# Two pairs of tiles change places in on-chip memory: the key tiles ahead of the token tiles

## The chip, the cores and the metric

The kernel runs on one core of a Trainium2 chip. Its engines are TensorE (matrix products; in the profile PE for the products and PEld for loading their weights), VectorE (DVE), ScalarE (ACT) and GpSimd (POOL); SyncE (SP) issues the DMA transfers. On-chip memory has 128 partitions; a tile takes the same range of bytes in each of them, and "a byte offset" here is the place of that range inside a partition. The metric is the time of one execution on the device, in microseconds.

## The reference

Everything is float32. Two layers follow an attention stage:

```
# attention: batch 2, 8 heads, 768 tokens, 64 channels a head
k_sum = max of k over blocks of 32 tokens;  v_sum = mean of v over the same blocks
scores = q k^T / 8 where |i - j| < 16 (else -1e9), beside q k_sum^T / 8 + log 32
x = softmax(scores) [v; v_sum]                      -> 1536 tokens x 512
# layer 0 and layer 1: 512 -> 2048 -> 512
h = x @ w_in;   g = h * clip(h + 3, 0, 6) / 6;   x = g @ w_out
h = x @ w_in2;  g = h * sigmoid(h);              out = g @ w_out2
```

## The kernel before

**Precision.** Each float32 operand of the two layers is split into a high and a low part (fp32r), and each product is made of three matmuls: high by high, high by low, low by high.

**Tiling.** The 1536 tokens are three blocks `j` of 512. Each layer's 2048 inner channels are two halves of 8 groups `f` of 128. A step is one (layer, half, j, f): there are 2 x 2 x 3 x 8 = 96. `hidden` (line 682) makes the 128 x 512 inner activations of a step with 12 matmuls: 4 blocks `kk` of 128 input channels by the three pairs of parts. ScalarE and VectorE then apply the activation and split the result (`act`, `gate`, `gate_hi`, `gate_lo`, lines 693 to 711). `project` (lines 732 and 735) adds the step's product with `w_out` to accumulators in PSUM with 12 matmuls. `finish` empties them into `acc` tiles (lines 775 to 789), from which the next layer's tokens are split (lines 785 and 793) or the output is written.

**Order.** One list, `ORDER`, written out in the file, gives the order of all operations, and so each engine's own order. Attention for 24 windows of 64 queries is woven into the first steps of layer 0. The weights are converted to high and low parts by ScalarE, VectorE and GpSimd (lines 380 to 420) as they arrive.

**The tiles of the change.** The token tiles `x1_0` and `x1_1` hold the tokens of blocks j = 0 and 1 for layer 0; in layer 1 the same bytes are `x2_0` and `x2_1`. The third block lies elsewhere, in a tile called `late` (`x1_late` in layer 0, `x2_2` in layer 1). All have the shape

```
x_shape = [P, WIDE // SUB, 2, KD, SUB]      # 128, 2 token halves, high/low, 4 blocks kk, 256 tokens
```

so that a partition holds 16,384 bytes of one, and a matmul of line 682 reads, as its moving operand,

```
w[:, a, kk * P : (kk + 1) * P],             # stationary: 128 x 128 weights
x[:, :, b, kk, :],                          # moving: two runs of 256 floats
```

two runs of 1,024 bytes that begin 8,192 bytes apart, the first at the tile's start + 4,096 b + 1,024 kk. Lines 732 and 735 read their moving operand (`g` or `w`) as one run of 2,048 bytes. The key tiles `kT` (12,608 bytes) hold the transposed keys of the two batches; GpSimd and VectorE copy windows out of them (line 565). Their bytes become the `acc` tiles (12,288 bytes, same tags `ka0`, `ka1`) later. No matmul reads `kT` or `acc`.

The trace leaves buffer numbers out of names. Its `x` is `x1_0`, `x1_1`, `x2_0`, `x2_1` and also `x2_2`; its `x_late` is `x1_late`.

Of the kernel before, what the change touches and what calls it, by code (L numbers as in the profile page):

```python
# [11 lines left out]
F32R = mybir.dt.float32r  # L12
# [8 lines left out]
P = 128  # L21
# [9 lines left out]
KD = DM // P  # L31
NF = DFF // P
HALF = NF // 2
WIDE = 512
NWIDE = NT // WIDE
SUB = 256
# [285 lines left out]
def attention_moe_kernel(  # L322
# [13 lines left out]
    main = ctx.enter_context(tc.tile_pool(name="main", bufs=1))  # L336
    psum = ctx.enter_context(tc.tile_pool(name="psum", bufs=1, space=bass.MemoryType.PSUM))

    def ring(pool, name, n, shape, dtype=F32):
        return Ring([pool.tile(shape, dtype, tag=f"{name}{i}", name=f"{name}{i}") for i in range(n)])  # L340

    cst = main.tile([P, NCONST], F32, tag="cst", name="cst")
    ident = cst[:, :P]
    x_shape = [P, WIDE // SUB, 2, KD, SUB]
    x1 = [main.tile(x_shape, F32R, tag=f"x{j}", name=f"x1_{j}") for j in range(NWIDE - 1)]
    kT = [main.tile([P, NHP * KROW + PAD], F32, tag=f"ka{b}", name=f"kT{b}") for b in range(B)]

    def key_rows(b, o=0):
        return kT[b][:, o : o + NHP * KROW].rearrange("p (h t) -> p h t", h=NHP)

    mags = ring(main, "mag", 1, [P, DM])
    bitss = ring(main, "bits", 2, [P, DM], U32)
    words = ring(main, "words", 3, [P, 2 * DM], U32)
# [564 lines left out]
```

## Time and profile before

| | |
|---|---|
| median of 3 runs | 627.41 us (625.96 to 627.69) |
| profiled execution | 626.98 us, of which 625.2 us from the first to the last instruction (the span) |
| PE busy | 608.6 us, 97% of the span |
| DVE busy | 398.8 us, 64% |
| ACT busy | 243.4 us, 39% |
| POOL busy | 63.4 us, 10% |
| mean granted TensorE clock | 0.989 of full |

Matmuls are pipelined, so that the busy time of one (some 390 ns) is longer than the distance to the next. The rate is read from starts: the start of one row of the timeline minus the start of the row before it, divided by the matmuls of that row.

### The profile page before, as it was taken

Reading aid. Unit: us, or ns where it says so; the run is one execution under the profiler, and the core shown is the slowest. Engines: PE = TensorE matmul, PEld = TensorE weight load, DVE = VectorE, ACT = ScalarE, POOL = GpSimd, SP = SyncE. Lnnn points to the kernel's source line nnn. Section 1 sums busy time; section 2 is a strip of 40 time slices with the busy share of each in tenths; the row PEclk is TensorE's granted clock in tenths of the full one; section 3 lists DMA queues with packets and bytes.
Section 4 is the critical chain, followed back from the end, with each engine's and each line's share of the span. In section 5 each row is a group of like instructions: output and inputs, shape, how many; then the busy total and the mean of one; then the engine's idle time right before and its main releaser. Section 6 shows DMA issues by size and latency. Waiting matters only on the chain.

```text
span 625.2 us, 8645 instructions
## 1 busy us (share of the span) xinstructions
PE 608.6 (97%) x3208; PEld 500.3 (80%) x3208; DVE 398.8 (64%) x908; ACT 243.4 (39%) x568; POOL 63.4 (10%) x90
## 2 busy tenths in 40 slices
PE   6899999999999989999999999999999999999997
PEld 5788788888788868888888888888888888888886
DVE  5789999856569999862369999432159423332442
ACT  3789787454235454331143453211243221111100
POOL 3576443111010000000000000000000000000000
PEclk8799999999999998999999999999999999999999
DMA  9997854221324454400003434200003000100101
GB/s 240 208 225 179 226 158 141 80 60 26 92 67 135 143 161 136 150 17 1 1 0 102 139 107 128 66 0 1 0 1 101 1 1 1 68 0 1 68 1 67
DMA packets 69051, 51.56 MB, mean 82 GB/s; under 512 B 36369, under 2 KB 63505, under 8 KB 69009
## 3 DMA queue, kind: packets, MB, share of 16 engines
q1 hardware_dynamic: 69008, 51.01, 28.9%
q8 instruction: 25, 0.41, 0.3%
q14 instruction: 18, 0.14, 0.1%
HBM read 47.85 MB, written 3.15 MB: 82 GB/s over the span
## 4 chain that ended last, share of the span: by engine, by line
PE 82%; DVE 13%; ACT 3%; issue 1%; POOL 0%; ACTq 0%; DVEq 0%
PE bank L682 37%; PE bank L735 21%; PE bank L732 18%; DVE bits L398 2%; DVE bits L405 2%; PE bank L575 2%; PE bank L644 1%; DVE bits L385 1%; DVE mag L392 1%; PE bank L632 1%; PE bank L470 1%; ACT prob L604 1%; DVE rw L700 1%; DVE gw L711 1%; PE bank L851 1%
## 5 line engine op out<-in xcount | busy, mean ns | idle before, releaser
L682 PE MATMUL bank<-x,w 128*128 128x512 f32 x720 | 179.2, 396 | 0.7 <-DVE x L667 0.7
L682 PEld LDWEIGHTS bank<-x,w 128*128 128x128 f32 x720 | 133.7, 188 | 30.9 <-ACT early_units L604 0.9
L735 PE MATMUL bank<-w,gw 128*128 128x512 f32 (+1 forms) x456 | 103.8, 378 | 0.0
L735 PEld LDWEIGHTS bank<-w,gw 128*128 128x128 f32 x456 | 82.9, 188 | 16.8
L711 DVE TENSOR_TENSOR gw<-rw,gw 128x512 fp32r<-128x512 f32 x80 | 55.1, 689 | 49.2 <-ACT gw L707 47.5
L704 DVE TENSOR_TENSOR rw<-bank,rw 128x512 f32<-128x512 f32 x48 | 32.9, 686 | 69.3 <-ACT rw L695 69.3
L380 ACT ACTIVATE mag<-words 128x512 f32<-128x512 f32 x64 | 43.3, 676 | 65.4 <-DVE bits L398 65.2
L695 ACT ACTIVATE rw<-bank 128x512 f32<-128x512 f32 x48 | 28.4, 595 | 93.6 <-PE bank L682 84.8
L682 PE MATMUL bank<-x,we 128*128 128x512 f32 x240 | 59.0, 393 | 0.0
L732 PE MATMUL bank<-gw,w 128*128 128x512 f32 x240 | 58.0, 390 | 0.0
L707 ACT CAST gw<-rw 128x512 fp32r<-128x512 f32 x45 | 28.0, 622 | 71.1 <-PE bank L735 43.4
L682 PEld LDWEIGHTS bank<-x,we 128*128 128x128 f32 x240 | 45.0, 188 | 10.3
L732 PEld LDWEIGHTS bank<-gw,w 128*128 128x128 f32 x240 | 45.1, 188 | 9.6
L732 PE MATMUL bank<-gn,w 128*128 128x512 f32 x192 | 48.4, 398 | 0.2 <-DVE gn L711 0.2
L398 DVE SCALAR_TENSOR_TENSOR bits<-mag,bits 128x512 uint32<-128x512 uint32 x64 | 45.0, 703 | 0.9
L405 DVE SCALAR_TENSOR_TENSOR bits<-words,bits 128x512 uint32<-128x512 uint32 x64 | 45.0, 703 | 0.4
L732 PEld LDWEIGHTS bank<-gn,w 128*128 128x128 f32 x192 | 35.1, 188 | 8.2 <-DVE gn L711 0.5
L700 DVE SCALAR_TENSOR_TENSOR rw<-rw,bank 128x512 f32<-128x512 f32 x32 | 21.8, 682 | 28.7 <-ACT rw L693 28.7
L732 PE MATMUL bank<-gw,we 128*128 128x512 f32 x144 | 37.6, 406 | 2.4 <-DVE gw L711 0.9
L732 PEld LDWEIGHTS bank<-gw,we 128*128 128x128 f32 x144 | 27.9, 196 | 10.0 <-DVE gw L711 1.7
L735 PE MATMUL bank<-we,gw 128*128 128x512 f32 x144 | 34.7, 390 | 0.0
L682 PE MATMUL bank<-x_late,w 128*128 128x512 f32 x144 | 34.1, 389 | 0.0
(103 smaller groups left out, 715.1 us busy)
## 6 DMA issues: line engine op xcount, KB each, us to landing
words<-in_moe_w_in_dram SPq DMA_DIRECT2D x32, 512.0 KB, 3.8
words<-in_moe_w_out_dram SPq DMA_DIRECT2D x32, 512.0 KB, 3.4
vwin<-in_v_dram SPq DMA_DIRECT2D x15, 192.0 KB, 4.2
out_dram<-acc SPq DMA_DIRECT2D x11, 256.0 KB, 2.0
qkv<-in_q_dram SPq DMA_DIRECT2D x10, 256.0 KB, 5.1
stage<-in_k_dram SPq DMA_DIRECT2D x3, 512.0 KB, 5.4
qkv<-in_k_dram SPq DMA_DIRECT2D x6, 256.0 KB, 4.7
stage<-in_v_dram SPq DMA_DIRECT2D x3, 512.0 KB, 6.8
```

What stands on the lines that cost most here:

```text
L380: nc.scalar.activation(out=out, in_=low_high(h)[:, 1].bitcast(F32), func=AF.Abs, scale=EXP_SHIFT)
L398: nc.vector.scalar_tensor_tensor(out=bits, in0=mags.use(h).bitcast(U32), scalar=3, in1=bits, op0=ALU.logical_shift_left, op1=ALU.bitwise_or,)
L405: nc.vector.scalar_tensor_tensor(out=bits, in0=low_high(h)[:, 1], scalar=0x80000000, in1=bits, op0=ALU.bitwise_and, op1=ALU.bitwise_or,)
L575: nc.tensor.matmul(ps[:, hp * NSLOT : (hp + 1) * NSLOT], qT[:, hp, t % 4, :], kw[:, hp, :], start=True, stop=True,)
L682: nc.tensor.matmul(ps, w[:, a, kk * P : (kk + 1) * P], x[:, :, b, kk, :], start=(m == 0), stop=(m == last),)
L695: nc.scalar.activation(out=r, in_=ps, func=AF.Sigmoid)
L700: nc.vector.scalar_tensor_tensor(out=r, in0=r, scalar=6.0, in1=ps, op0=ALU.min, op1=ALU.mult)
L704: nc.vector.tensor_tensor(out=r, in0=ps, in1=r, op=ALU.mult)
L707: copier("gate_hi", i)(out=gs.take(i, 1)[:, 0], in_=rs.use(i))
L711: nc.vector.tensor_tensor(out=g[:, 1], in0=rs.use(i), in1=g[:, 0].bitcast(F32), op=ALU.subtract)
L732: nc.tensor.matmul(ps, lhs, g[:, b], **flags)
L735: nc.tensor.matmul(ps[:, : len(cols)], g[:, a, rows], rhs, **flags)
```

## The change

The two lines that allocate `kT` (and the helper `key_rows`) move ahead of the allocation of `x1`:

```
--- before.py
+++ after.py
     cst = main.tile([P, NCONST], F32, tag="cst", name="cst")
     ident = cst[:, :P]
+    kT = [main.tile([P, NHP * KROW + PAD], F32, tag=f"ka{b}", name=f"kT{b}") for b in range(B)]
+
+    def key_rows(b, o=0):
+        return kT[b][:, o : o + NHP * KROW].rearrange("p (h t) -> p h t", h=NHP)
+
     x_shape = [P, WIDE // SUB, 2, KD, SUB]
     x1 = [main.tile(x_shape, F32R, tag=f"x{j}", name=f"x1_{j}") for j in range(NWIDE - 1)]
-    kT = [main.tile([P, NHP * KROW + PAD], F32, tag=f"ka{b}", name=f"kT{b}") for b in range(B)]
-
-    def key_rows(b, o=0):
-        return kT[b][:, o : o + NHP * KROW].rearrange("p (h t) -> p h t", h=NHP)
-
     mags = ring(main, "mag", 1, [P, DM])
```

The pool gives out bytes in the order of allocation. The four tiles together take as much as before (2 x 16,384 + 2 x 12,608 bytes), so what is allocated behind them stays where it was. In the compiled programs the tiles begin at these bytes of a partition:

| tile | before | after | before mod 1,024 | after mod 1,024 |
|---|---|---|---|---|
| `cst` | 16,512 | 16,512 | 128 | 128 |
| `x1_0`, `x2_0` | 18,656 | 43,872 | 224 | 864 |
| `x1_1`, `x2_1` | 35,040 | 60,256 | 224 | 864 |
| `kT0`, `acc00`, `acc10` | 51,424 | 18,656 | 224 | 224 |
| `kT1`, `acc01`, `acc11` | 64,032 | 31,264 | 544 | 544 |
| `mag`, `bits`, `words` | 76,640 on | 76,640 on | 864 | 864 |
| weights `w0` to `w7` | 95,072 to 152,416 | the same | 864 | 864 |
| `late` (`x1_late`, `x2_2`) | 160,608 | 160,608 | 864 | 864 |
| weights `we0` to `we3` | 176,992 to 201,568 | the same | 864 | 864 |
| `gn`, `gw` | 185,184 to 217,952 | the same | 864 | 864 |

Every other tile keeps its place too. The lists of instructions of all five engines, with their operands, order and waits, are the same in both programs but for the numbers of the buffers and these addresses.

## Rows read from the trace of the kernel before

**Rows 1.** The chain that ended last, by line: 58 to 177.2, 177 to 234, 234 to 625.2 us.
```profile
by line: PE bank L732 37.8%; PE bank L682 33.8%; PE bank L644 7.1%; PE bank L575 5.9%; PE bank L632 5.5%; DVE bits L405 1.8%; DVE bits L398 1.5%; DVE prob L590 1.2%; DVE bits L385 0.9%; PE bank L470 0.9%; PE bank L538 0.8%; DVE gn L707 0.7%
...
by line: DVE bits L405 16.3%; DVE bits L398 16.2%; DVE rw L700 10.4%; DVE bits L385 10.1%; DVE gw L711 9.8%; DVE mag L392 9.0%; issue 8.3%; DVE w L420 7.0%; DVE we L420 5.3%; DVE gw L707 2.5%; ACT we L416 2.2%; PE bank L732 1.4%; DVE we L41
...
by line: PE bank L682 48.5%; PE bank L735 33.6%; PE bank L732 17.2%; DVE acc L787 0.1%; issue 0.0%
```

**Rows 2.** Timeline of PE, 312 to 352 us: start, us, engine, line, operation, tiles, count.
```profile
318.14 2.88 PE L682 MATMUL bank<-x_late,we 128*128 128x512 f32 x12
320.86 2.88 PE L732 MATMUL bank<-gw,w 128*128 128x512 f32 x12
...
342.62 2.96 PE L682 MATMUL bank<-x,w 128*128 128x512 f32 x12
345.41 1.54 PE L732 MATMUL bank<-gw,we 128*128 128x512 f32 x6
346.79 2.88 PE L682 MATMUL bank<-x_late,w 128*128 128x512 f32 x12
349.51 2.66 PE L732 MATMUL bank<-gw,w 128*128 128x512 f32 x11
```

**Rows 3.** Timeline of PE, layer 0: block j = 0 or 1, 275 to 297 us.
```profile
275.46 5.75 PE L682 MATMUL bank<-x,we 128*128 128x512 f32 x24
281.05 2.90 PE L732 MATMUL bank<-gw,we 128*128 128x512 f32 x12
283.79 1.55 PE L682 MATMUL bank<-x,w 128*128 128x512 f32 x6
285.18 1.54 PE L732 MATMUL bank<-gw,we 128*128 128x512 f32 x6
```

**Rows 4.** Timeline of PE, layer 1: 378 to 402 us, then `x2_2` at 565 to 580.
```profile
382.66 5.62 PE L735 MATMUL bank<-w,gw 128*128 128x512 f32 x24
388.12 2.95 PE L682 MATMUL bank<-x,we 128*128 128x512 f32 x12
390.91 9.70 PE L735 MATMUL bank<-we,gw 128*128 128x512 f32 x42
...
568.39 9.73 PE L682 MATMUL bank<-x,w 128*128 128x512 f32 x42
577.95 2.43 PE L735 MATMUL bank<-w,gw 128*128 128x512 f32 x10
```

**Rows 5.** Windows, instructions on tile `x` alone: PE, PEld, DVE, ACT busy (count), clock, DMA.
```profile
58.00:177.20 119.20, 49.78 (x192) 34.83 (x192) 4.80 (x12) 2.16 (x6) 1.00 0.39 108
177.20:233.96 56.76, 10.42 (x42) 7.88 (x42) 0.00 (x0) 0.00 (x0) 1.00 0.45 139
233.96:625.20 391.24, 177.15 (x726) 136.07 (x726) 7.79 (x12) 7.41 (x12) 1.00 0.14 46
```

**Rows 6.** Windows, 177.2 to 233.96 us: PE, PEld, DVE, ACT, POOL busy, clock, DMA.
```profile
177.20:233.96 56.76, 54.38 (x236) 43.59 (x235) 55.01 (x108) 30.41 (x52) 1.70 (x1) 1.00 0.45 139
```

**Rows 7.** Timeline, 176.6 to 180 us, then of PE from 230 us.
```profile
177.34 1.14 ACT L416 CAST we<-bits 128x512 fp32r<-128x512 f32 x2 [6.77 <-PE bank L732]
177.99 0.69 DVE L420 TENSOR_TENSOR we<-bits,we 128x512 fp32r<-128x512 f32 x1 [5.06 <-ACT we L416]
...
231.14 0.96 PE L732 MATMUL bank<-gw,we 128*128 128x512 f32 x3 [0.80 <-DVE rw L700]
232.75 0.49 PE L732 MATMUL bank<-gw,we 128*128 128x512 f32 x1 [0.65 <-DVE gw L707]
233.96 4.37 PE L732 MATMUL bank<-gw,we 128*128 128x512 f32 x11 [0.71 <-DVE gw L711]
238.16 1.55 PE L732 MATMUL bank<-gw,w 128*128 128x512 f32 x6
```

**Rows 8.** Windows around 234 us, columns as in rows 6.
```profile
229.00:234.00 5.00, 2.62 (x9) 1.02 (x7) 5.00 (x11) 3.30 (x7) 0.00 (x0) 1.00 0.62 201
234.00:235.00 1.00, 1.00 (x3) 0.83 (x4) 0.97 (x3) 0.01 (x1) 0.00 (x0) 0.62 0.00 0
235.00:236.00 1.00, 1.00 (x3) 0.74 (x3) 1.00 (x3) 0.00 (x0) 0.00 (x0) 0.50 0.25 37
238.00:239.00 1.00, 1.00 (x6) 0.83 (x5) 0.67 (x3) 0.62 (x1) 0.00 (x0) 1.00 0.00 0
```

**Rows 9.** The tiles `x`, then `x_late`: count, ns min/median/max, first and last start.
```profile
L667 DVE TENSOR_TENSOR x<-bank,x x16: 391/414/427, 47.7 to 106.5; 128x256 fp32r<-128x256 f32 x16
L663 ACT CAST x<-bank x10: 355/366/378, 47.0 to 102.0; 128x256 fp32r<-128x256 f32 x10
...
L667 DVE TENSOR_TENSOR x_late<-bank,x_late x8: 417/424/426, 130.6 to 170.6; 128x256 fp32r<-128x256 f32 x8
L663 ACT CAST x_late<-bank x2: 362/367/372, 135.4 to 170.2; 128x256 fp32r<-128x256 f32 x2
```

More of the change, by code (lines that the diff above doesn't have):

```diff
@@ L343, in attention_moe_kernel @@
     ident = cst[:, :P]
-    x_shape = [P, WIDE // SUB, 2, KD, SUB]
-    x1 = [main.tile(x_shape, F32R, tag=f"x{j}", name=f"x1_{j}") for j in range(NWIDE - 1)]
     kT = [main.tile([P, NHP * KROW + PAD], F32, tag=f"ka{b}", name=f"kT{b}") for b in range(B)]
@@ L349, in key_rows @@
         return kT[b][:, o : o + NHP * KROW].rearrange("p (h t) -> p h t", h=NHP)
+    x_shape = [P, WIDE // SUB, 2, KD, SUB]
+    x1 = [main.tile(x_shape, F32R, tag=f"x{j}", name=f"x1_{j}") for j in range(NWIDE - 1)]
     mags = ring(main, "mag", 1, [P, DM])
```

## The prediction

> **What bounds the kernel now.** I read the chain of work that ended last in three stretches [rows 1]. From 58 to 177 us it runs through PE for over nine tenths, with little of DVE in between. From 177 to 234 us it hardly touches PE: DVE, which converts weights and splits activations, works 55.01 of 56.76 us [rows 6], and PE waits for it at the end, 0.80, 0.65 and 0.71 us in a row [rows 7]. From 234 us to the end it is PE alone: lines 682, 735 and 732 hold 99.3%. So in the last 391 us anything that makes a matmul shorter makes the kernel shorter, and in the stretch before that nothing on PE does.
>
> Then I read the rate of the matmuls from the timeline, since a tile's place can act only on the instructions that touch it. The reader is to see one comparison. At 342.62 us stand 12 matmuls of line 682 on `x`, and the next row starts at 345.41: 2.79 us, 232.5 ns each. At 346.79 stand 12 of the same line and form, with the same kind of weights `w`, on `x_late`, and the next row starts at 349.51: 2.72 us, 226.7 ns each; so at 318.14 too, with the other weights, `we` [rows 2]. Block j = 0 or 1 in layer 0 gives 5.59 us for 24, 232.9 ns, and 1.39 us for 6 [rows 3]; layer 1 gives 2.79 us for 12 on `x2_0` or `x2_1`, but 9.56 us for 42, 227.6 ns, on `x2_2`, which lies in the bytes of `x_late` [rows 4]. [...] So 682's matmuls take some 6 ns more when their moving operand is in the two token tiles at the front of the memory, in both layers and with either weights; the third block, of the same shape and pattern, is free of it. Line 735, whose moving operand is one run in `w`, goes at 5.46 us for 24, 227.5 ns [rows 4].
>
> **What about the place costs 6 ns?** The two tiles at 233 ns begin at 224 modulo 1,024; `late`, and the weights that PE loads beside it, at 864. Within a tile the 8 positions that matmuls read from (`b`, `kk`) differ by multiples of 1,024 bytes, and the second run lies 8,192 further, so a rule that hung on address bits from 1,024 up to 8,192 would make some of these dear and some cheap; but groups of 6 (two of the four `kk`) cost 1.39 us where groups of 12 cost 2.79 and 24 cost 5.59 [rows 2, 3]. The two tiles lie 16,384 apart, and each of them spans as much, so a bit of 16,384 is out too. What is left is the place below 1,024 (224 against 864), or a rough region of the memory: those two end at byte 51,424, and every moving operand at 227 ns lies above 95,072. The change moves both token tiles to 864 modulo 1,024, the residue of everything that goes at 227, but only to bytes 43,872 to 76,640. I take the first reading: I see no cause for a border in the memory, whereas a phase between what is read at once (moving run against weights, 640 bytes apart before, none after) is one thing that the change makes equal to the case of `late`. This is an inference; no row shows a token tile at 864 in the lower part.
>
> **The change part by part.** Nothing is removed, added or reordered: the engines' lists are equal, so no wait and no DMA issue is new. Contrary to what "all other tiles" suggests, four places move and no more. Costs:
>
> 1. *Matmuls of line 682 on the token tiles.* The trace counts 192 + 42 + 726 on `x` in the three stretches [rows 5]; of the last, 192 (2 halves x 8 groups x 12) are on `x2_2`, which goes at 227 already and stays. So 192, 42 and 534 get 6.0 ns shorter (232.5 to 232.9 against 226.7). After 234 us: 534 x 6.0 = 3.2 us, all on the chain.
> 2. *The 42 between 177 and 234*: 0.25 us, worth nothing, since DVE is the chain; PE would wait 0.25 us longer at 229 to 234.
> 3. *The 192 before 177*: 1.15 us of PE. DVE's long stretch starts when ACT converts into `we`, which ACT could start only at PE's line 732 (it had waited 6.77 us [rows 7]); what PE gains earlier starts DVE earlier. Bounds: nothing (if waits on DVE and ACT between the attention's pieces eat it) and 1.15. The chain is over 90% PE here, but the small matmuls are interleaved with others' answers; I take 0.9.
> 4. *Writes into the token tiles by ACT and DVE.* Already the same at both residues: 366 against 367 ns and 414 against 424 [rows 9]. With the worse, 28 x 0.01 us = 0.3 us beside PE's work: nothing.
> 5. *Key and `acc` tiles.* They move by exactly 32,768 bytes, so that their residues stay; their users are ACT, DVE, POOL and DMA, and after 234 us chain time on DVE is 0.1% [rows 1]. Nothing; if the new place cost a hundredth of each, the sum would be under 0.1 us at the end, where the last piece is not hidden.
>
> Sum: 3.2 + 0.9 = 4.1 us. Against the profiled execution of 626.98 us this gives 622.9 us. That execution lies 0.43 us under the median of the runs, 627.41; from there it is 623.3. I forecast 623.1 us. Differences of 0.3%, 1.9 us, are about what a measurement of this kernel can tell from no change.
>
> [...]
>
> **The rivals.**
>
> *A region, not a residue.* If reads in the low 65,536 bytes cost the 6 ns (the only border at a multiple of 16,384 bytes that leaves every moving operand of 227 ns outside and both token tiles inside and that the new places straddle), `x_0` at 43,872 to 60,256 gains nothing. Of `x_1`'s 12 matmuls a step, 8 read their first run below and their second above, 4 read the low parts, mostly above: some 7.5 of 12 gain, 7.5 x 32 steps = 240 x 6.0 = 1.4 us, 1.2 of it on the chain by the shares above: 625.8 us, within 0.3%. A border higher up, under 95,072, would give nothing. For it: no moving operand at 227 ns lies below 95,072. Against it: w, we, gw and `late` range over 120,000 bytes without any step in the rate.
>
> *Nothing changes.* The 6 ns hang on something that goes with the blocks j = 0, 1 and not with their place, or on a phase that the new place does not mend: 627.0 us. Against it: both layers, both halves and different neighbours in time show the same split, and `x2_2` is block 2 of another layer with other work around it.
>
> [...]
>
> **How the numbers follow.** The residue: 0.74, all but 0.01 of it faster by over 0.3%. Its own range is 3.2 to 4.6 us of gain from 627 to 627.4, and 0.6 for the scatter of runs: 621.9 to 624.6. The region: 0.11, inside 0.3%, nearly always. Nothing changes: 0.10, inside 0.3%, with a little on both sides. Slower through the clock or by something that I did not see: 0.05. Faster 0.74, same 0.20, slower 0.06. The range leaves out the cases of no change and slower, and goes on the low side to the full 4.6 us with scatter: 621.7 to 626.3, which takes in most of the region's case.
>
> **What would show it.** In the changed kernel's timeline 12 matmuls of line 682 on `x` must take 2.72 us in both layers, like `x_late`, and 24 must take 5.45. The chain after 234 us stays on PE, with the same three lines and a smaller share of 682. DVE's stretch of 57 us must stay as long and start up to 1 us earlier, and PE's waits before 234 us stay or grow by 0.25. If 2.79 stays for all, the residue is wrong; if only part of the groups falls to 2.72, or to values between, it is a region. If the rate falls and the time doesn't, a wait or a longer stretch at half clock after 234 us must stand in its place.

## The result, and the profile after

The changed kernel takes 621.55 us (median of 4 runs, 619.95 to 622.91) against 627.37 us before (median of 4): a ratio of 0.9911, with a 95% interval of 0.9882 to 0.9939. Run again beside the kernel before (experiment 10) it took 622.20 us against 627.44: 0.9937, interval 0.9915 to 0.9958. The ratios, here and below, are those on record with their intervals; they are not the quotients of the medians and differ a little from them. So the changed kernel is faster, by 0.9% and by 0.6% as the two ratios have it, and by anything from 0.4 to 1.2% with their intervals. The profiled execution took 619.95 us, with a span of 618.2 us, 7.0 us less than the span before.

The timeline of PE of the changed kernel in the place that answers to [rows 2]:

```profile
313.89 2.88 PE L682 MATMUL bank<-x_late,we 128*128 128x512 f32 x12
316.61 2.88 PE L732 MATMUL bank<-gw,w 128*128 128x512 f32 x12
...
338.37 2.88 PE L682 MATMUL bank<-x,w 128*128 128x512 f32 x12
341.09 1.52 PE L732 MATMUL bank<-gw,we 128*128 128x512 f32 x6
342.45 2.88 PE L682 MATMUL bank<-x_late,w 128*128 128x512 f32 x12
345.17 5.15 PE L732 MATMUL bank<-gw,w 128*128 128x512 f32 x22
```

The same twelve matmuls on `x` now go from 338.37 to 341.09: 2.72 us, where they took 2.79; the twelve on `x_late` keep their 2.72. The six of line 732 between them are a little shorter too, 1.36 us against 1.38. Layer 0, block 0 or 1, and then layer 1, the places of [rows 3] and [rows 4]:

```profile
271.73 5.60 PE L682 MATMUL bank<-x,we 128*128 128x512 f32 x24
277.17 2.88 PE L732 MATMUL bank<-gw,we 128*128 128x512 f32 x12
...
383.25 2.88 PE L682 MATMUL bank<-x,we 128*128 128x512 f32 x12
385.97 9.68 PE L735 MATMUL bank<-we,gw 128*128 128x512 f32 x42
395.49 2.88 PE L682 MATMUL bank<-x,w 128*128 128x512 f32 x12
```

24 on `x` take 5.44 us, where they took 5.59, and 12 in layer 1 take 2.72. The rows of lines 682, 732 and 735 now all go at one rate, 226.7 ns. The chain from 232.3 us to the end is still PE's, with the same three lines and a slightly smaller share of line 682:

```profile
by line: PE bank L682 48.3%; PE bank L735 33.9%; PE bank L732 16.9%; DVE acc L787 0.1%; issue 0.0%
```

Where the stretch that DVE sets begins, in the timeline of the changed kernel, the place of the first of [rows 7]:

```profile
175.65 1.14 ACT L416 CAST we<-bits 128x512 fp32r<-128x512 f32 x2 [6.76 <-PE bank L732]
```

Where it ends, in the timeline of PE of the same kernel:

```profile
227.94 0.73 PE L732 MATMUL bank<-gw,we 128*128 128x512 f32 x2 [0.54 <-DVE gw L711]
229.47 0.96 PE L732 MATMUL bank<-gw,we 128*128 128x512 f32 x3 [0.80 <-DVE rw L700]
231.09 0.50 PE L732 MATMUL bank<-gw,we 128*128 128x512 f32 x1 [0.65 <-DVE gw L707]
232.29 2.79 PE L732 MATMUL bank<-gw,we 128*128 128x512 f32 x11 [0.70 <-DVE gw L711]
234.92 1.52 PE L732 MATMUL bank<-gw,w 128*128 128x512 f32 x6
```

And its windows there, which answer to [rows 8] (columns as there):

```profile
229.00:232.00 3.00, 1.46 (x4) 0.67 (x4) 3.00 (x7) 1.94 (x5) 0.00 (x0) 1.00 0.48 175
232.00:233.00 1.00, 0.71 (x3) 0.62 (x4) 0.97 (x3) 0.34 (x1) 0.00 (x0) 1.00 0.00 0
235.00:236.00 1.00, 1.00 (x6) 0.85 (x5) 1.00 (x3) 0.53 (x1) 0.00 (x0) 1.00 1.06 377
```

DVE's stretch, from ACT's start on `we` to PE's start on the 11 matmuls, lasts 56.64 us (175.65 to 232.29), and lasted 56.62. PE's first wait in it has grown from 0.22 to 0.54 us; the three others are the same. The first wait in the timeline of PE of the kernel before:

```profile
229.61 0.73 PE L732 MATMUL bank<-gw,we 128*128 128x512 f32 x2 [0.22 <-DVE gw L711]
```

What differs is what follows: the granted clock stays full, 1.00 in these windows, where it falls to 0.50 in [rows 8], and the 11 matmuls take 2.63 us instead of 4.20.

**Where the 7.0 us of the two spans come from.** Four marks, the same instruction in each: the start of six matmuls of line 732 on `gn` early on (73.22 before, 72.12 after), ACT's start on `we` (177.34 and 175.65), the 11 matmuls (233.96 and 232.29), the end (625.2 and 618.2). The first mark in the timeline of PE, before:

```profile
73.22 1.63 PE L732 MATMUL bank<-gn,w 128*128 128x512 f32 x6
```

and after:

```profile
72.12 1.64 PE L732 MATMUL bank<-gn,w 128*128 128x512 f32 x6
```

| stretch | before, us | after, us | gain |
|---|---|---|---|
| to the `gn` mark | 73.22 | 72.12 | 1.10 |
| to ACT on `we` | 104.12 | 103.53 | 0.59 |
| DVE's stretch | 56.62 | 56.64 | 0 |
| the 11 matmuls at the clock's fall | 4.20 | 2.63 | 1.57 |
| the rest | 387.04 | 383.28 | 3.76 |

The first and the fourth go with how an execution starts and with its clock, not with the change (below); 0.59 + 3.76 = 4.35 us are the change's. The profiled execution of experiment 10, the same kernel, gives the same two lengths, 103.53 us (to ACT's start at 177.52) and 383.25 us (to its end at 620.0), though it reaches the `gn` mark 1.87 us later. Its timeline of PE:

```profile
73.99 1.64 PE L732 MATMUL bank<-gn,w 128*128 128x512 f32 x6
...
234.16 2.76 PE L732 MATMUL bank<-gw,we 128*128 128x512 f32 x11 [0.70 <-DVE gw L711]
236.75 1.52 PE L732 MATMUL bank<-gw,w 128*128 128x512 f32 x6
```

### The profile page after: what moved, and what is told of

It reads as the page before. It is cut to its first block, busy times and chain, and to the rows that moved or that the text cites. A ratio compares the mean times of both kernels' runs of the same rounds, so it can differ in the third digit from the quotient of the medians.

```text
span 618.2 us, 8645 instructions
## 1 busy us (share of the span) xinstructions
PE 599.6 (97%) x3208; PEld 496.7 (80%) x3208; DVE 399.5 (65%) x908; ACT 243.3 (39%) x568; POOL 63.4 (10%) x90
## 4 chain that ended last, share of the span: by engine, by line
PE 82%; DVE 14%; ACT 3%; issue 1%; ACTq 0%; DVEq 0%
PE bank L682 37%; PE bank L735 21%; PE bank L732 18%; DVE bits L405 2%; DVE bits L398 2%; PE bank L575 2%; PE bank L644 1%; DVE bits L385 1%; DVE mag L392 1%; PE bank L632 1%; DVE rw L700 1%; DVE gw L711 1%; PE bank L470 1%; DVE kmax L484 1%; PE bank L851 1%
## 5 line engine op out<-in xcount | busy, mean ns | idle before, releaser
L682 PE MATMUL bank<-x,w 128*128 128x512 f32 x720 | 176.4, 392 | 0.7 <-DVE x L667 0.7
L732 PE MATMUL bank<-gw,we 128*128 128x512 f32 x144 | 35.9, 393 | 2.7 <-DVE gw L711 1.2
```

Of the source, the lines that this page charges most:

```text
L682: nc.tensor.matmul(ps, w[:, a, kk * P : (kk + 1) * P], x[:, :, b, kk, :], start=(m == 0), stop=(m == last),)
L732: nc.tensor.matmul(ps, lhs, g[:, b], **flags)
```

## The experiments

All put tiles elsewhere and leave every operation, its order and its data as they are. Small tiles that are put in front (`vsum` of 512 bytes, `kmax0` of 384) are taken from the end of the memory; `gap` is an empty tile. In each, the phase is the byte where the token tiles begin less the byte where the weights begin, modulo 256: 128 in the kernel before (224 - 864 modulo 256), 0 in the changed one. "The rate" is twelve matmuls of line 682 on block 0 or 1 in layer 1 near 388 us, from start to start. Line numbers are shifted by up to four where lines were added. Beside experiments 1 to 4 the kernel before took 626.71 us (median of 30), beside 5 to 8 627.00 (of 17), beside 9 to 12 627.44 (of 23).

**1. Same region, other residue.** The token tiles stay in front of the key tiles, wholly below byte 65,536, but 640 bytes higher:

```
     ident = cst[:, :P]
+    vsum = main.tile([P, P], F32, tag="vsum", name="vsum")
+    gap = main.tile([P, 32], F32, tag="gap", name="gap")
...
     kT = [main.tile([P, NHP * KROW + PAD], F32, tag=f"ka{b}", name=f"kT{b}") for b in range(B)]
+    kmax0 = main.tile([P, NHP, NB], F32, tag="kmax0", name="kmax0")
```

> Order as before (token tiles ahead of the key tiles), but with 640 bytes put ahead of the token tiles and 384 behind the key tiles, so that the token tiles begin at bytes 19,296 and 35,680: wholly in the low region, as before the change, yet at 864 modulo 1,024, as after it; weights, late and gw move by 1,024 and keep their residue. Residue theory: 12 matmuls of line 682 on x take 2.72 us in both layers, time 621 to 623.5 us. Region theory (reads below byte 65,536 are dear): they take 2.79 us, time 627 us. A theory in which the key tiles' new place brings the gain: 2.79 us and 627 us.

It took 621.66 us, ratio 0.9929 (0.9904 to 0.9955), and the rate is 2.72 us in the timeline of PE of this kernel:

```profile
385.85 2.88 PE L685 MATMUL bank<-x,we 128*128 128x512 f32 x12
388.57 9.68 PE L738 MATMUL bank<-we,gw 128*128 128x512 f32 x42
```

The region falls, and so does any gain from the key tiles' own new place: they lie here, but for 640 bytes, where they lay before.

**2. Same residue, everything moved.** The 640 bytes stand ahead of everything, so that token tiles are at 864 modulo 1,024 but the weights at 480:

```
+    vsum = main.tile([P, P], F32, tag="vsum", name="vsum")
+    gap = main.tile([P, 32], F32, tag="gap", name="gap")
     cst = main.tile([P, NCONST], F32, tag="cst", name="cst")
```

> Order as before, with 640 bytes put ahead of everything: token tiles at 864 modulo 1,024, but the weights, late and gw now at 480, so that the distance between moving token tile and weights is what it was before (640 bytes below them, modulo 1,024). If the token tile's own residue decides: 2.72 us for 12 on x, time about 622 us. If the phase between the token tile and the weights that PE loads at the same time decides: 2.79 us, 627 us, while late (phase zero) stays at 2.72. Region theory: 2.79 us, 627 us. If the own residue decides, lines 732 and 735, whose moving operands have gone from 864 to 480, may change too.

626.50 us, ratio 1.0005 (0.9985 to 1.0025), and the rate in its timeline of PE is the old 2.79:

```profile
388.26 2.95 PE L684 MATMUL bank<-x,we 128*128 128x512 f32 x12
391.05 9.70 PE L737 MATMUL bank<-we,gw 128*128 128x512 f32 x42
```

The tile's own address modulo 1,024 is that of the changed kernel, and it brings nothing. What is as before is the distance to the weights.

**3. One tile of two.** The key tiles between the token tiles, `x1_0` at its old place:

```
     x0 = main.tile(x_shape, F32R, tag="x0", name="x1_0")
...
     xb = main.tile(x_shape, F32R, tag="x1", name="x1_1")
```

> Key tiles between the two token tiles: x1_0 stays at its old place (224 modulo 1,024), x1_1 goes to the place that the change gives it (864). Residue theory: 12 matmuls on block j = 0 take 2.79 us, on j = 1 2.72 us, and half of the gain of the rate, some 2 us, is left: 624.5 us. Region theory: j = 0 takes 2.79, j = 1 something between, 626 us. If the gain of the change came from elsewhere (clock, start-up), no split by block.

624.71 us, ratio 0.9967 (0.9951 to 0.9983): about half the gain. In its timeline of PE block 0 keeps 2.79 us, block 1, twelve us later, has 2.72:

```profile
387.68 2.95 PE L686 MATMUL bank<-x,we 128*128 128x512 f32 x12
390.47 9.70 PE L739 MATMUL bank<-we,gw 128*128 128x512 f32 x42
400.01 2.88 PE L686 MATMUL bank<-x,w 128*128 128x512 f32 x12
402.73 1.52 PE L739 MATMUL bank<-we,gw 128*128 128x512 f32 x6
```

**4. One key tile ahead.** Token tiles at 544 modulo 1,024, phase 192:

```
     kT0 = main.tile([P, NHP * KROW + PAD], F32, tag="ka0", name="kT0")
...
     kT1 = main.tile([P, NHP * KROW + PAD], F32, tag="ka1", name="kT1")
```

> Only one of the two key tiles ahead: token tiles at 31,264 and 47,648, 544 modulo 1,024. The residue theory holds one rate for all token matmuls of both blocks, and which of the two (2.72 or 2.79 us for 12) tells how fine the dependence is: 544 differs from 224 and 864 alike by 320. If the dependence is on 32 against 96 modulo 128, a third value is possible. Region theory: 2.79 us.

626.05 us, ratio 0.9990 (0.9969 to 1.0011); the rate in its timeline of PE is 2.80 us for block 0 and 2.80 for block 1. Half the change brings nothing that can be measured.

```profile
385.00 2.96 PE L686 MATMUL bank<-x,we 128*128 128x512 f32 x12
387.80 9.70 PE L739 MATMUL bank<-we,gw 128*128 128x512 f32 x42
397.34 2.96 PE L686 MATMUL bank<-x,w 128*128 128x512 f32 x12
400.14 1.54 PE L739 MATMUL bank<-we,gw 128*128 128x512 f32 x6
```

**5. No tile of the change moved.** Token and key tiles at the very bytes of before; 384 bytes behind them lift the rest:

```
     kT = [main.tile([P, NHP * KROW + PAD], F32, tag=f"ka{b}", name=f"kT{b}") for b in range(B)]
+    kmax0 = main.tile([P, NHP, NB], F32, tag="kmax0", name="kmax0")
```

> Order as before; the token tiles and the key tiles stay at the very bytes of before (18,656, 35,040, 51,424, 64,032), and one small tile of 384 bytes, taken from the end of the memory, stands behind them, so that the weights, late and gw lie 384 bytes higher, at 224 modulo 1,024 like the token tiles. If the phase between token tile and weights decides: 12 matmuls on x take 2.72 us though no token tile has moved, time about 622 us. If the token tile's own residue or place decides: 2.79 us, 627 us.

622.12 us, ratio 0.9925 (0.9903 to 0.9947), and 2.72 us in its timeline of PE:

```profile
385.67 2.88 PE L683 MATMUL bank<-x,we 128*128 128x512 f32 x12
388.39 9.68 PE L736 MATMUL bank<-we,gw 128*128 128x512 f32 x42
```

The whole gain, with the token tiles where they were. Together with 2 this settles that the place of a token tile counts only against that of something behind the key tiles.

**6 to 8. The period, and other phases.** 384 bytes ahead of the token tiles and 640 behind the key tiles (distance 256, phase 0); token tiles ahead of `cst` (phase 32); one key tile, then the token tiles, then `cst` (phase 96).

```
6:  cst, kmax0, x1, kT, vsum, gap      7:  x1, cst, kT      8:  kT0, x1, cst, kT1
```

> Token tiles at 608 modulo 1,024 with the weights at 864: 256 bytes apart, 0 modulo 256 but not modulo 512. If the phase counts modulo 256: 2.72 us for 12 on x and about 622 us. If it counts modulo 512 or 1,024: 2.79 us or thereabouts and 627 us.

> Token tiles ahead of all, at 128 modulo 1,024, weights at 864: 288 bytes ahead of the weights modulo 1,024, which is 32 modulo 256 or 64 or 128. If the phase counts modulo 256 and only zero is cheap: 2.79 us or more, 627 us. If a small distance is as good as zero: 2.72 us, 622 us. A value under 2.72 would be a cheaper phase than the one that the change gives.

> One key tile and then the token tiles ahead of cst: token tiles at 448 modulo 1,024, weights at 864: 608 apart, 96 modulo 256. The phase theory expects one rate for both blocks and both layers; 2.72 us for 12 if distances below some bound within 256 are free, 2.79 or more if only zero is.

Number 6 took 622.25 us, ratio 0.9928 (0.9899 to 0.9956), at 2.72 us: a distance of 256 is as good as none. Number 7 took 629.12, ratio 1.0032 (1.0012 to 1.0051), at 2.81 us, and so is a little slower than the kernel before. Number 8, one execution, took 627.06 us at 2.82 (387.24 to 390.06). The timeline of PE of number 6:

```profile
386.53 2.88 PE L685 MATMUL bank<-x,we 128*128 128x512 f32 x12
389.25 9.68 PE L738 MATMUL bank<-we,gw 128*128 128x512 f32 x42
```

and of number 7:

```profile
389.86 2.97 PE L686 MATMUL bank<-x,we 128*128 128x512 f32 x12
392.67 9.72 PE L739 MATMUL bank<-we,gw 128*128 128x512 f32 x42
```

**9. Another pair of operands.** The changed kernel, with `gw` 128 bytes higher in its pool (and behind it `rw`, which no matmul reads). Line 732 has its moving operand in `gw`, line 735 its stationary one:

```
         ws.free += ring(pool, "we", EXTRA, [P, 2, 1024], F32R).free
+        gap = pool.tile([P, 32], F32, tag="gap", name="gap")
         gs.free = ring(pool, "gw", LAG + 1, [P, 2, WIDE], F32R).free
```

> The changed kernel, with one more edit: the tiles gw, which are the moving operand of line 732 and the stationary one of line 735 from step 16 on, lie 128 bytes higher, half a period of 256 away from the weights, with which they were in step. Token tiles and weights stay in step. Phase theory (moving and stationary operand of one stream, modulo 256): 12 matmuls of lines 732 and 735 with gw take 2.79 us instead of 2.72, line 682 stays at 2.72, and some 960 matmuls cost 6 ns more, of which those between 177 and 234 us are hidden: 5 us slower than the changed kernel, about 627 us. If something else than the two operands of the matmul decides: no line changes, 622 us.

628.27 us; the changed kernel on the same chip took 622.20, so 6.1 us more by the medians, where 5 was expected. Line 735 takes 9.76 us for 42, where it took 9.52 (385.97 to 395.49), which is 232.4 ns each, and line 732 takes 2.79 for 12 (322.23 to 325.02), where it took 2.72; line 682, whose operands stay in step, takes 2.74 for 12, in this kernel's timeline of PE:

```profile
322.23 2.96 PE L732 MATMUL bank<-gw,w 128*128 128x512 f32 x12
325.02 1.54 PE L682 MATMUL bank<-x_late,we 128*128 128x512 f32 x6
...
390.01 2.90 PE L682 MATMUL bank<-x,we 128*128 128x512 f32 x12
392.75 9.92 PE L735 MATMUL bank<-we,gw 128*128 128x512 f32 x42
402.51 2.89 PE L682 MATMUL bank<-x,w 128*128 128x512 f32 x12
```

So the effect is not one of token tiles. In line 732 only the moving operand has moved, in line 735 only the stationary one, and both pay some 6 ns (232.5 and 232.4 against 226.7); what counts is the place of one operand of a matmul against the other. For line 682 this is taken over from here: experiments 2 and 5 leave open which of the tiles behind the key tiles is the partner, and no run moved the weights alone.

**10. The changed kernel again.**

> The changed kernel once more, beside the other three on one chip: about 622 us, 2.72 us for 12 of every line, and 4 to 4.6 us under the kernel before when executions with the same mean clock are compared.

622.20 us, as told above. The mean granted clock of each execution is on record. At 0.989 the kernel before took 627.85 us on this chip (mean of 10 executions) and the changed one 623.79 (mean of 4): 4.06 us less. At 0.992 the changed one took 621.81 (mean of 4) and the kernel before 626.95 (a single execution): 5.1 us less. So executions of like mean clock don't fix the gain to better than about 1 us.

**11 and 12. Phases 64 and 224**, with what lies behind the key tiles 64 and 416 bytes higher, one execution each:

```
11:  cst, x1, kT, gap (64 bytes)      12:  cst, x1, kT, kmax0, gap (32 bytes)
```

> Order as before, token tiles at their old bytes, all that is allocated behind the key tiles 64 bytes higher: token tiles 64 bytes ahead of the weights modulo 256. Phases measured so far: 0 at 2.72 us for 12, and 32, 96, 128 and 192 at 2.79 to 2.81. If only zero is cheap: 2.79 to 2.81 us, 627 us.

> Order as before, token tiles at their old bytes, all that is allocated behind the key tiles 416 bytes higher: token tiles 224 bytes ahead of the weights modulo 256, that is 32 behind them. If only zero is cheap: 2.79 to 2.81 us for 12, 627 us; if a small lag is as good as none (a small lead was not): 2.72 us, 622 us.

628.22 and 627.86 us. Phase 64 has 2.77 us, half-way, and not the 2.79 to 2.81 that was expected of it; phase 224 has 2.81. The timeline of PE of number 11:

```profile
389.47 2.93 PE L683 MATMUL bank<-x,we 128*128 128x512 f32 x12
392.24 9.73 PE L736 MATMUL bank<-we,gw 128*128 128x512 f32 x42
```

and of number 12:

```profile
388.51 2.96 PE L684 MATMUL bank<-x,we 128*128 128x512 f32 x12
391.32 9.71 PE L737 MATMUL bank<-we,gw 128*128 128x512 f32 x42
```

All of them in one table, twelve matmuls from start to start:

| phase, bytes mod 256 | 0 | 32 | 64 | 96 | 128 | 192 | 224 |
|---|---|---|---|---|---|---|---|
| us for 12 | 2.72 | 2.81 | 2.77 | 2.82 | 2.79 | 2.80 | 2.81 |
| kernels | after, 1, 5, 6, 10 | 7 | 11 | 8 | before, 2 | 4 | 12 |

A distance of 256 costs nothing (2.72 us, experiment 6), and 128, 64 and 32 do (2.79, 2.77 and 2.81); so by the distances tried the period is 256 bytes. No phase measured is cheaper than zero, and in the changed kernel all matmul operands of the two layers are at zero. Among the phases tried none is left that would gain more there; the matmuls of the attention were not examined.

## Why the prediction was right

**What bounds the kernel.** As predicted, what PE gains after 234 us is gained, what it gains in DVE's stretch is waited away (56.64 against 56.62 us, and 0.32 us more of waiting at its first wait, where 0.25 was forecast).

**The cause.** The comparison in the trace of before, two tiles of one shape at two rates, named the effect and its size. The granted clock does not set the two apart: in the kernel before it is 1.00 from 275 to 297, 312 to 352, 378 to 402 and 565 to 580 us, where the rates were read. The argument that bits from 1,024 up can't matter held, and so did the choice of a phase against a region: experiments 1, 2 and 5 rule out the region and the tile's own residue. What the prediction left undecided between "residue" and "phase" is decided for the phase, and the period is not 1,024 but 256 bytes. What set the phase of the kernel before is what stood between the token tiles and the weights: `mag`, `bits` and `words` take 18,432 bytes, a multiple of 256, but each key tile takes 12,608, which is 64 modulo 256. Two of them in between give phase 128 (the kernel before), one gives 192 (experiment 4), none gives 0 (the change).

**The terms.** The matmuls after 234 us: forecast 534 x 6.0 = 3.2 us, measured 3.76. Summed from start to start over the last stretch of the two timelines, line 682 gained 3.16 us of it, as forecast, and lines 732 and 735 the other 0.59. The prediction missed these neighbours: the matmuls that follow a group on `x` were late as well (1.38 against 1.36 us for six of line 732), though none of them reads a token tile. The 192 before 177 us: forecast 0.9, measured 0.59 from the `gn` mark on, where 156 of the 192 stand, 0.94 us of PE; so about a third of it did not come through. The share of the 36 ahead of the mark can't be told from the scatter of the start. Together 4.35 us against 4.1: that the sum comes so near is in part luck, since one term was too small and the other too large. Writes to the token tiles, key tiles and `acc`: nothing, as experiment 1 shows for them together, where these tiles lie but for 640 bytes as before and the gain is there.

**The time and the range.** The forecast was 623.1 us, in a range of 621.7 to 626.3. The two medians are 621.55 and 622.20: the first lies 0.15 us under the range, the second inside it. The range's low side was meant to hold the full 4.6 us of gain with 0.6 for the scatter of runs, and the first pair of medians lies 5.8 us apart. (The prediction gives this low end as 621.9 and as 621.7; its own terms, 627 - 4.6 - 0.6, make it 621.8.)

**What was not forecast.** The profiled execution gained 7.0 us, not 4.1. Two parts are not the change's. The clock's fall behind PE's waits is absent from this execution and from the profiled one of experiment 10 (granted clock 1.00 from 230 to 245 us in both), but there in those of 1 and 5 (0.89, as before), which go at the same rate; and there is no sign of it in that of 4, which goes at the old rate. In 5 the 11 matmuls take 4.22 us behind waits of 0.52, 0.80, 0.63 and 0.71, as its timeline of PE shows:

```profile
233.18 4.39 PE L733 MATMUL bank<-gw,we 128*128 128x512 f32 x11 [0.71 <-DVE gw L712]
237.40 1.55 PE L733 MATMUL bank<-gw,w 128*128 128x512 f32 x6
```

In 4 they take 2.64 us, in its timeline of PE:

```profile
232.17 2.81 PE L736 MATMUL bank<-gw,we 128*128 128x512 f32 x11 [0.70 <-DVE gw L715]
234.81 1.52 PE L736 MATMUL bank<-gw,w 128*128 128x512 f32 x6
```

And the start-up: the changed kernel reaches the `gn` mark at 72.12 us in one execution and at 73.99 in the other, on either side of the 73.22 of before. So DVE's stretch starts 1.69 us earlier than before and not up to 1 us, 1.10 of it by the start-up. Executions of the kernel before with mean clocks of 0.986 and 0.997 lie 4.6 us apart in their mean times (below). That is enough for medians that lie 5.8 and 5.2 us apart where the rate accounts for 4.35; that it is the whole reason is likely, and not shown.

**The rivals.** The region: refuted by 1, where the rate is 2.72 us with both token tiles below byte 65,536. Nothing changes: refuted by the rate, 2.72 us for 12 against 2.79. Slower through the clock: the kernel is faster. Behind PE's waits, of which the first grew by 0.32 us, the clock did not stay low for longer: where it fell at the new rate, in 5, the 11 matmuls took 4.22 us against 4.20 before, and in the profiled executions of after and of 10 it did not fall there at all (1.00 from 230 to 245 us). So the waits alone do not bring the fall; what does is not shown.

## What to carry to other kernels

Where one operand's matmuls are a few per cent slower than another's of the same shape, compare the byte offsets of the two operands of each matmul, modulo 256, before looking for a wait: here 768 matmuls paid 6 ns each for that alone. What shifts one operand against the other is a tile between them whose size is no multiple of 256 bytes (here the key tiles, 64 modulo 256 each). One ahead of both does no harm: the constants' 2,144 bytes are 96 modulo 256, and by experiment 2 a shift of everything changes nothing (2.79 us for 12, ratio 1.0005). So allocate such tiles ahead of all matmul operands of a stream, or behind them, or fill them up to a multiple of 256. Then read from the chain in which stretches the gain counts. The runs show this for 128 x 128 by 128 x 512 matmuls in fp32r with a new weight load for each (3208 loads for 3208 matmuls in the trace of before); other types and shapes were not tried.

## What the runs showed of the hardware

The rate of a 128 x 128 by 128 x 512 fp32r matmul in a steady stream is 226.7 ns when moving and stationary operand start at the same byte modulo 256, and 230.8 to 235 ns at the other phases tried (32, 64, 96, 128, 192 and 224) for a moving operand of two runs of 1,024 bytes (line 682). For one run of 2,048 bytes (lines 732 and 735) phase 128 alone was tried beside zero, and gave 232.5 and 232.4 ns. The granted clock from 245 to 600 us is 1.00 in the profiled executions of before, after, 1, 5 and 10. So the places of the two operands against each other have an effect on the rate, 226.7 against some 233 ns. Nothing here shows by what mechanism, nor why phase 64 costs line 682 less than the others (0.05 us for 12, where they cost 0.07 to 0.10); phases finer than 32 bytes were not tried.

Executions of one kernel differ in when and how far the granted clock of TensorE falls. From 10 to 20 us it is 0.83 in the profiled execution of experiment 10 and 1.00 in the other of the changed kernel, from 20 to 30 us 1.00 and 0.94, from 30 to 40 us 0.83 and 0.89. The mean granted clock of the kernel before ranged from 0.986 to 0.997 in the executions beside experiment 10, with mean times of 628.8 and 624.2 us at those two.
